# Start addresses of TensorE's operands in SBUF: streamed tiles at 0 and held tiles at 128 modulo 256 bytes, in place of 0 and 64 modulo 128

## The chip, the cores and the metric

The kernel runs on one core of a Trainium2 chip. The metric is the device time of one execution in microseconds (us), and the time of a kernel is the median of several executions. TensorE (PE in the profile) multiplies, with its weight loads shown apart as PEld. VectorE (DVE), ScalarE (ACT) and GpSimd (POOL) do the elementwise work, and SyncE (SP) issues most of the DMAs.

## The reference

A gated linear attention over 4 batches, 8 heads, 768 steps and head size 48, followed by a two-layer feed-forward block with an exact GELU (3072 tokens, 384 wide, 2048 hidden). All arrays are float32.

```
state = 0                                   # [B, H, 48, 48]
for t in range(768):
    state = alpha[t, :, None] * state + outer(k[t], v[t])
    y[t] = q[t] @ state
x = y as [3072, 384]
h = x @ w_in                                # [3072, 2048]
g = 0.5 * h * (1 + erf(h / sqrt(2)))
out = g @ w_out                             # [3072, 384]
```

## The kernel before, in words

**Attention.** The 768 steps are cut into blocks of 256 tokens, 12 blocks in all, each with two units of four heads (24 units). In a unit VectorE makes running products of alpha by scans (L339, L352) and scales queries and keys with them. TensorE then makes scores (L379), the products inside a chunk of 64 steps (L469), the sums of keys and values (L488) and what the carried state adds (L546). These are float32 matmuls on 64 by 64 or 48 by 48 corners of the array. Their operands are the tiles `qd`, `kd`, `vn`, `ss`, `kn` and `states`.

**Feed-forward.** A float32 matrix is split into a high and a low part in the format float32r, and a product is made of three matmuls: high by high, low by high, high by low. The weights are `wih`, `wil` (w_in, high and low) and `woh`, `wol` (w_out). The attention's output, split, is the tile `x` (in the program's names `x0`, `x3`, `x4`, `x6`, `x10`, or `two_x`). Every matmul loads 128 columns of the one operand as weights and streams the other.

- Narrow blocks, 0 to 3, have 256 tokens. The first product (L665) holds `wih`/`wil` and streams 256 columns of `x`. Blocks 0 and 3 read `x0` and `x3`, blocks 1 and 2 `two_x`. The second product (L886) holds the GELU's output, `ghi` or `glo`, and streams 384 columns of `woh` or `wol`.
- Wide blocks, four of them, have 512 tokens. The first product (L681) holds `wih`/`wil` and streams 512 columns of `x` (blocks 4, 6 and 10) or `two_x` (block 8). The second product holds `woh`/`wol` and streams 512 columns of `ghi`/`glo` (L696).
- From the second wide block on most of the second product is made by a scheme with fewer multiplications (L790). It streams `ghi`/`glo` or a difference of them, which lies in the places of `qd0` and `ad1`. As weights it holds `woh`/`wol` or sums of those, which lie in room that other tiles left (`sums_x`, `sums_kn`, `sums_ss`, `sums_z`, `sums_pp`, `sums_rp`, and the tiles `x0`, `qd1`, `kd1`).

In the program these are 576 matmuls of L665 (256 columns), 384 of L886 (384 columns), 432 of L681 on `x4`, `x6` and `x10` and 144 on `two_x`, 180 of L696 (512 columns each), and 132 of 512 and 462 of 256 columns of L790: 2,310 in all. Each is issued right behind the last one. The weights of the next one are loaded while this one streams.

**Order.** A planner in the kernel places every step by a table of costs (`COST`) and due times and writes out the order of all engines by hand. Addresses don't enter it. Tiles lie in SBUF pools in the order in which they are asked for, and `gap` asks for an unused tile where an address is to be moved on.

**Addresses.** A tile begins at the same byte in every one of the 128 partitions. `gap(pool, name, size)` takes `size % LINE` bytes. Before, `LINE` is 128 and the offsets are these:

```
STREAM, HELD, X_AT = 0, 64, 0
LINE = 128
```

Of the kernel before, what the change touches and what calls it, by code (L numbers as in the profile page):

```python
# [8 lines left out]
F32 = mybir.dt.float32  # L9
F32R = mybir.dt.float32r  # L10
# [33 lines left out]
    hi=0.82, lo=0.89, gemm1=2.12, gelu=0.51, low=0.62, most=1.4, last=0.69, part=1.0,  # L44
    wide1=2.1, wide2=2.07, wpart=1.1, quick1=2.45, quick2=1.42, comb1=0.36, comb3=1.08, chi=0.98, clo=1.2, wsum=0.72, wcomb=0.52, whi=0.52, wlo=0.65, gather=1.7, keep=0.95, evac=1.45, wend0=1.38, wend1=2.76, fsum=0.4, fall=0.2, fout=0.2,
)
STREAM, HELD, X_AT = 0, 64, 0
LINE = 128
ORDER = "0 1 a b c 2 d 3 e f 4 g h i j k 5 l m n o p"


# [1 line left out]
def gla_then_gelu_ffn(ctx: ExitStack, tc: tile.TileContext, q, k, v, alpha, qg, kg, ag, vg, w_in, w_out, out):  # L53
    nc = tc.nc
    B, H, D, S = q.shape
    NF, P, NK, _ = w_in.shape
    DM, DFF = NK * P, NF * P
    NT = B * S
    C = 128
    G = 2 * C  # L60
# [13 lines left out]
    A_MAX = 1.04  # L74
    MID, BOTTOM = 2.0**53, 2.0**-80

    def gap(pool, name, size):

        if size % LINE:
            pool.tile([C, size % LINE // 4], F32, tag=f"gap_{name}", bufs=1, name=f"gap_{name}")  # L80

    const = ctx.enter_context(tc.tile_pool(name="const", bufs=1))
    work = ctx.enter_context(tc.tile_pool(name="work", bufs=3))
    ffn = ctx.enter_context(tc.tile_pool(name="ffn", bufs=2))
# [5 lines left out]
    first = first_cm.__enter__()  # L90
# [27 lines left out]
    W = 2 * G  # L118
# [43 lines left out]
    bottom = column("bottom", BOTTOM).to_broadcast([P, G])  # L162
    outside = const.tile([P, 3 * NG * NU], F32, name="outside")
    ends = const.tile([P, NG * NU, 2], F32, name="ends")
    gap(const, "data", STREAM - 64)

    NB = 2

    def data_tile(n, i, dtype=F32):
        return const.tile([P, NPAIR, G], dtype, tag=f"{n}d{i}", name=f"{n}d{i}")  # L170

    vbuf = []
    data = []
    for i in range(NB):
        vbuf.append(const.tile([P, NCH, HV * D + DR], F32, name=f"vn{i}"))
        data.append({"a": data_tile("a", i)})
        gap(const, f"k{i}", (HELD - STREAM) * i)
        data[i].update({n: data_tile(n, i) for n in "kq"})

    states = []  # L180
    for u in range(NU):
# [29 lines left out]
    parts_all = const.tile([P, NSB, 2, DM], F32, name="parts")  # L211
    parts = [parts_all[:, i] for i in range(NSB)]
    LONG = NK * 2 * G
    gap(const, "x0", X_AT - HELD)
    x0_room = const.tile([P, LONG + LINE // 4], F32R, name="x0")
    x0 = x0_room[:, :LONG].rearrange("p (n h t) -> p n h t", n=NK, h=2)
    gap(const, "minus", HELD - X_AT)

    edge = ctx.enter_context(tc.tile_pool(name="edge", bufs=1, side="right"))
    gap(edge, "edge", 96 - X_AT)  # L220
    stage_cm = tc.tile_pool(name="stage", bufs=STAGE, side="right")
    stage = stage_cm.__enter__()
    late = []
# [35 lines left out]
    minus = const.tile([P, P], F32R, name="minus")  # L259
# [303 lines left out]
    def block_of(g):  # L563
        return next((pair for pair in WIDE if g in pair), g)

    later = []

    def x_pool():
        if not later:
            early_cm.__exit__(None, None, None)  # L570
            later.append(ctx.enter_context(tc.tile_pool(name="later", bufs=1)))
            gap(later[0], "two_x", X_AT - STREAM)
        return later[0]

    def two_x():
        if len(later) < 2:
            later.append(x_pool().tile([P, NK * 2 * W], F32R, name="two_x"))
        return later[1]

    def x_tiles(g):  # L580
        pair = block_of(g)
        if pair == g:
            if g == NSB:
                x = late[0].tile([P, LONG + LINE // 4], F32R, tag="xn", bufs=1, name=f"x{g}")
                x = x[:, :LONG].rearrange("p (n h t) -> p n h t", n=NK, h=2)
            else:
                x = x0 if g in (0, "s") else two_x().rearrange("p (g n h t) -> p g n h t", g=2, n=NK, h=2)[:, g - 1]
            xt[g] = x[:, :, 0], x[:, :, 1]
            return x
        if pair not in xt:  # L590
            if pair == WIDE[2]:
                x = two_x().rearrange("p (n j h t) -> p n j h t", n=NK, j=2, h=2)
            else:
                x = late[0].tile([P, NK, 2, 2, G], F32R, tag="xl", name=f"x{g}")
            xt[pair] = x
        h = pair.index(g)
        return xt[pair][:, :, h]
# [19 lines left out]
    def x_tile(g):  # L617
        if (g, "x") not in cur:
            cur[g, "x"] = x_tiles(g)
            if g:  # L620
                cur[g, "z"] = ffn.tile([P, 2, G], F32R, tag="z", bufs=1, name=f"z{g}")
            else:
                cur[g, "z"] = ffn.tile([P, 2, G], F32, tag="z", bufs=1, name="z0")[:, 0]
# [90 lines left out]
    rooms = []  # L714

    def room_of():

        if not rooms:
            x3 = late[0].tile([P, LONG + LINE // 4], F32R, tag="xn", bufs=1, name="sums_x")
            first = (HELD - X_AT) % LINE // 4  # L720
            rooms.extend(x[:, first + i * 2 * G : first + (i + 1) * 2 * G] for x in (x0_room, x3) for i in range(NK))
        elif len(rooms) == 2 * NK:
            for n, i in (("q", 1), ("k", 1)):
                x = taken(n, i).rearrange("p n t -> p (n t)")
                rooms.extend((x[:, : 2 * G], x[:, 2 * G :]))
            for pool, tag, bufs in ((work, "kn", 2), (work, "kn", 2), (work, "ss", 1), (ffn, "z", 1), (work, "pp", 1), (work, "rp", 1)):
                rooms.append(pool.tile([P, 2 * G], F32R, tag=tag, bufs=bufs, name=f"sums_{tag}"))
        return rooms[2 * len(sums) : 2 * len(sums) + 2]
# [6 lines left out]
    def taken(n, i):  # L735
        quick.setdefault("taken", []).append((n, i))
        return data_tile(n, i, F32R)

    def w_sums(f2):
        places = room_of()  # L740
        sums[f2] = [x.rearrange("p (n e) -> p n e", n=4) for x in places]
        nc.vector.tensor_tensor(
            out=plain[:, :4].rearrange("p (f e) c -> p f (e c)", f=2),
            in0=wo_hi[f2][:, :, : 2 * P].bitcast(F32),
            in1=wo_lo[f2][:, :, : 2 * P].bitcast(F32),
            op=ALU.add,
        )
# [162 lines left out]
    def general_path():  # L910
# [77 lines left out]
        def narrow_block(n0):  # L988
            x = x_tiles("s")
            for c in range(2):  # L990
                x_again(x, n0, c, slice(c * C, (c + 1) * C))
            acc = [ps_o().tile([P, DM], F32, tag=f"acc{t}", name=f"acc{t}_s") for t in range(2)]
            for f in range(NF2):
                hp = gemm1("s", f)
                gh = gelus("s", f, hp)
                gl = gelu_low("s", f, hp, gh)
                evacuate = gemm2("s", f, gh, gl, acc, f == 0, f == NF2 - 1, f == NF2 - 1, n0)
            evacuate()
# [207 lines left out]

    total = const.tile([P, 1], F32, name="total")
    flag = const.tile([1, 1], I32, name="flag")
    gap(const, "work", HELD)
    gap(ffn, "ffn", STREAM - HELD)  # L1210

    def flag_sum():
        nc.vector.tensor_scalar(
# [353 lines left out]
    t = 0.0  # L1567
    idle = 0
    while True:
# [17 lines left out]
        t = min(later_on)  # L1587
# [92 lines left out]
```

## Time and profile before

| | |
|---|---|
| median of 3 executions | 482.35 us (482.22 to 483.43) |
| the profiled execution | 482.24 us |
| its span, first to last instruction | 480.7 us |
| TensorE busy | 470.0 us, 98% of the span |
| TensorE's weight loads busy | 412.3 us |
| VectorE busy | 340.6 us, 71% |
| ScalarE busy | 228.2 us, 47% |
| share of TensorE in the chain that ended last | 93% |

The chain that ended last is followed back from the last instruction of the program. Each of its pieces names the engine, the tile written, the line and the number of instructions. Where matmuls stand back to back in it, the length of a piece divided by its count is the time from the start of one matmul to the start of the next. I call that the spacing. The time that the profile gives for one matmul alone is longer than the spacing, since matmuls are pipelined.

### The profile page before, as it was taken

What the parts mean: (1) busy time and instruction counts of PE and PEld (TensorE: products, weight loads), DVE (VectorE), ACT (ScalarE), POOL (GpSimd) and SP (SyncE); (2) the same over time, 40 slices, a digit from 0 to 9 for tenths busy, and PEclk for the clock granted to TensorE, in tenths of its full rate; (3) what the DMA queues carried; (4) which work ended last, traced back from release to release, by engine and by line L of the source; (5) the groups of instructions that cost most, each with busy time, mean ns of one, the idle gap of its engine ahead of it and who ended that gap; (6) DMA issues with size and microseconds to landing.
All of it is one profiled execution on the core that took longest, in us unless ns stands there. A gap on an engine that the chain in (4) does not pass through costs nothing.

```text
span 480.7 us, 12552 instructions
## 1 busy us (share of the span) xinstructions
PE 470.0 (98%) x5328; PEld 412.3 (86%) x5328; DVE 340.6 (71%) x666; ACT 228.2 (47%) x429; POOL 7.4 (2%) x21
## 2 busy tenths in 40 slices
PE   7999999999999999999999999999999999999994
PEld 5688999999999999887778878888888888888883
DVE  6899899987977978788882354797474545654542
ACT  5898676353544344535343244454443343523341
POOL 2000000000000000000000000000000000000000
PEclk9999999999999999999999999999999999999998
DMA  7997654557656554646340040000010000010002
GB/s 298 400 388 244 220 180 167 166 174 188 219 169 192 175 171 148 195 148 214 96 148 10 22 138 31 1 0 1 1 65 2 1 0 1 0 67 0 2 1 73
DMA packets 33921, 56.68 MB, mean 118 GB/s; under 512 B 3744, under 2 KB 13280, under 8 KB 33856
## 3 DMA queue, kind: packets, MB, share of 16 engines
q1 hardware_dynamic: 32400, 50.94, 32.3%
q0 software_dynamic: 880, 3.93, 2.1%
q8 instruction: 44, 0.72, 0.6%
q10 hardware_dynamic: 576, 0.92, 0.5%
q14 instruction: 21, 0.17, 0.1%
HBM read 43.45 MB, written 12.32 MB: 116 GB/s over the span
## 4 chain that ended last, share of the span: by engine, by line
PE 93%; DVE 3%; DMA 1%; issue 1%; ACT 0%; SPq 0%; DVEq 0%
PE hw L681 28%; PE acc L886 14%; PE hp L665 13%; PE accw L790 11%; PE accw L696 9%; PE sbank L790 6%; PE sbank L469 2%; PE sbank L546 2%; PE sbank L488 2%; DMA two_x<-zd 1%; PE sh L379 1%; DVE pp L339 1%; PE ybank L546 1%; DVE rp L352 1%; PE sbank L379 1%
## 5 line engine op out<-in xcount | busy, mean ns | idle before, releaser
L681 PE MATMUL hw<-x,wih 128*128 128x512 f32 x288 | 89.8, 393 | 0.0
L861 ACT ACTIVATE ghi<-hw 128x512 fp32r<-128x512 f32 x64 | 38.2, 597 | 91.0 <-PE hw L681 88.8
L876 DVE TENSOR_TENSOR glo<-h,ghi 128x512 fp32r<-128x512 f32 x44 | 30.1, 688 | 52.9 <-ACT h L866 52.9
L681 PEld LDWEIGHTS hw<-x,wih 128*128 128x128 f32 x288 | 52.0, 188 | 9.9
L681 PE MATMUL hw<-x,wil 128*128 128x512 f32 x144 | 56.6, 393 | 0.0
L783 ACT CAST qd<-ad 128x1024 fp32r<-128x1024 f32 x22 | 23.1, 1052 | 45.6 <-DVE ad L780 45.6
L886 PE MATMUL acc<-woh,ghi 128*128 128x384 f32 x128 | 44.1, 344 | 0.0
L886 PE MATMUL acc<-wol,ghi 128*128 128x384 f32 x128 | 43.0, 336 | 0.0
L786 DVE TENSOR_TENSOR ad<-ad,qd 128x1024 fp32r<-128x1024 f32 x22 | 26.9, 1224 | 18.7 <-ACT qd L783 18.7
L861 ACT ACTIVATE ghi<-hp 128x512 fp32r<-128x512 f32 x32 | 19.1, 596 | 42.5 <-PE hp L665 42.3
L665 PE MATMUL hp<-x,wih 128*128 128x256 f32 x192 | 35.0, 282 | 0.0
L665 PE MATMUL hp<-two_x,wih 128*128 128x256 f32 x192 | 34.4, 281 | 0.4 <-DMA two_x<-zd 0.4
L352 DVE TENSOR_TENSOR_SCAN rp<-ad,rp,bottom 128x255 f32<-128x255 f32 x48 | 34.1, 739 | 0.9
L339 DVE TENSOR_TENSOR_SCAN pp<-ad,bottom 128x256 f32<-128x256 f32 x48 | 30.7, 666 | 3.7 <-DMA ad<-in_ag_dram 3.7
L681 PEld LDWEIGHTS hw<-x,wil 128*128 128x128 f32 x144 | 27.0, 188 | 6.1
L665 PEld LDWEIGHTS hp<-two_x,wih 128*128 128x128 f32 x192 | 29.8, 188 | 0.6 <-PE hp L665 0.6
L681 PE MATMUL hw<-two_x,wih 128*128 128x512 f32 x96 | 30.1, 395 | 0.0
L665 PEld LDWEIGHTS hp<-x,wih 128*128 128x128 f32 x192 | 29.7, 188 | 0.2
L876 DVE TENSOR_TENSOR glo<-hw,ghi 128x512 fp32r<-128x512 f32 x20 | 13.8, 688 | 21.4 <-ACT hw L866 21.2
L886 PE MATMUL acc<-woh,glo 128*128 128x384 f32 x128 | 28.4, 344 | 0.0
L665 PE MATMUL hp<-two_x,wil 128*128 128x256 f32 x96 | 26.9, 280 | 0.0
L665 PE MATMUL hp<-x,wil 128*128 128x256 f32 x96 | 26.7, 280 | 0.0
(268 smaller groups left out, 1105.6 us busy)
## 6 DMA issues: line engine op xcount, KB each, us to landing
st<-in_moe_w_in_dram SPq DMA_DIRECT2D x8, 768.0 KB, 7.5
st<-in_moe_w_out_dram SPq DMA_DIRECT2D x8, 768.0 KB, 6.5
qd<-in_qg_dram SPq DMA_DIRECT2D x23, 256.0 KB, 3.5
ad<-in_ag_dram SPq DMA_DIRECT2D x23, 256.0 KB, 3.6
kd<-in_kg_dram SPq DMA_DIRECT2D x23, 256.0 KB, 4.5
vn<-in_vg_dram SPq DMA_DIRECT2D x12, 416.0 KB, 6.3
fd<-fl SPq DMA_DIRECT2D x18, 256.0 KB, 2.1
kx<-fd SPq DMA_DIRECT2D x72, 64.0 KB, 3.2
```

The lines of the kernel that those rows point to most:

```text
L339: nc.vector.tensor_tensor_scan(pp[:, i], at[:, i], bottom, MID, ALU.mult, ALU.max)
L352: nc.vector.tensor_tensor_scan(rp[:, i, G - 2 :: -1], at[:, i, G - 1 : 0 : -1], bottom[:, 1:], rp[:, i, G - 1 :], ALU.mult, ALU.max)
L546: ins = nc.tensor.matmul(ybank[o, i, t], lhsT=states[u][r, j, i], rhs=d["qt"][r, i, t], start=False, stop=True, skip_group_check=True,)
L665: nc.tensor.matmul(hp[:, j, :], lhsT=a[:, j, i * P : (i + 1) * P], rhs=x[:, i, :], start=(start and m == 0), stop=(stop and (j, i, n) in t ...
L681: nc.tensor.matmul(hp, lhsT=a[:, j, i * P : (i + 1) * P], rhs=x[:, i, :, part], start=(i == 0 and n == 0), stop=(i == NK - 1 and n == 2),)
L696: nc.tensor.matmul(acc[i], lhsT=w[:, j, e], rhs=a, start=(f == 0 and k == 0 and w is wo_hi[f2]), skip_group_check=mixed, stop=(f == NF - 1 ...
L783: nc.scalar.copy(quick["hi"], quick["t"])
L786: nc.vector.tensor_tensor(out=quick["lo"], in0=quick["t"], in1=quick["hi"].bitcast(F32), op=ALU.subtract)
L790: nc.tensor.matmul(to, lhsT=a[x], rhs=b[y], start=(start and n == 0), stop=True, skip_group_check=True)
L861: nc.scalar.activation(ghi, hp, AF.Gelu)
L876: nc.vector.tensor_tensor(out=glo, in0=hp, in1=ghi.bitcast(F32), op=ALU.subtract)
L886: nc.tensor.matmul(acc[t], lhsT=a[:, j, t * C : (t + 1) * C], rhs=w[:, j, :], start=(first and j == 0 and k == 0 and w is wo_hi[f]), stop= ...
```

## The change

It renames and refines the offsets, makes them count modulo 256 bytes, and puts gaps where they are needed for it. The core of the diff:

```diff
-STREAM, HELD, X_AT = 0, 64, 0
-LINE = 128
+LINE = 256
+GELU_AT, HELD_AT, COMB_AT, WIDE_AT, NARROW_AT = 0, 128, 0, 0, 0
...
-    gap(const, "data", STREAM - 64)
+    gap(const, HELD_AT - 192)
...
-        data.append({"a": data_tile("a", i)})
-        gap(const, f"k{i}", (HELD - STREAM) * i)
-        data[i].update({n: data_tile(n, i) for n in "kq"})
+        data.append({})
+        for n in "akq":
+            if (n, i) in (("q", 0), ("a", 1)):
+                gap(const, (COMB_AT - HELD_AT) * (i == 0))
+            data[i][n] = data_tile(n, i)
+            if (n, i) == ("a", 1):
+                gap(const, HELD_AT - COMB_AT)
...
-    gap(const, "x0", X_AT - HELD)
-    x0_room = const.tile([P, LONG + LINE // 4], F32R, name="x0")
-    x0 = x0_room[:, :LONG].rearrange("p (n h t) -> p n h t", n=NK, h=2)
-    gap(const, "minus", HELD - X_AT)
+    def long_tile(pool, name, **kw):
+        return pool.tile([P, LONG + LINE // 4], F32R, name=name, **kw)
+
+    def narrow_x(t):
+        at = (NARROW_AT - HELD_AT) % LINE // 4
+        return t[:, at : at + LONG].rearrange("p (n h t) -> p n h t", n=NK, h=2)
+
+    x0_room = long_tile(const, "x0")
+    x0 = narrow_x(x0_room)
...
-    gap(edge, "edge", 96 - X_AT)
+    gap(edge, 224 - WIDE_AT)
...
-            gap(later[0], "two_x", X_AT - STREAM)
+            gap(later[0], WIDE_AT - GELU_AT)
...
-            later.append(x_pool().tile([P, NK * 2 * W], F32R, name="two_x"))
+            later.append(x_pool().tile([P, 2 * LONG + LINE // 4], F32R, name="two_x"))
...
-            first = (HELD - X_AT) % LINE // 4
-            rooms.extend(x[:, first + i * 2 * G : first + (i + 1) * 2 * G] for x in (x0_room, x3) for i in range(NK))
+            rooms.extend(x[:, i * 2 * G : (i + 1) * 2 * G] for x in (x0_room, x3) for i in range(NK))
...
-    gap(const, "work", HELD)
-    gap(ffn, "ffn", STREAM - HELD)
+    gap(const, -64)
+    gap(ffn, GELU_AT - HELD_AT)
```

The order of instructions stays as it is: on each of the five engines the two programs agree row by row. Only addresses move. This is where tiles begin modulo 256 bytes, from the two built programs (slices that matmuls take of a float32r tile are whole multiples of 512 bytes apart, so that they keep its residue):

| tile | used as | before | after |
|---|---|---|---|
| `wih`, `wil`, `woh`, `wol` | weights (L665, L681, L696, L790), streamed in L886 | 64 | 128 |
| `ghi`, `glo` | streamed (L696, L790), weights in L886 | 0 | 0 |
| `x4`, `x6`, `x10` | streamed (L681) | 128 | 0 |
| `two_x` | streamed (L665, L681) | 0 | 0 |
| `x0` as streamed | L665, block 0 | 128 | 0 |
| `x3` as streamed | L665, block 3 | 0 | 0 |
| `qd0`, `ad1` | streamed differences (L790) | 0 | 0 |
| sums in `x0`, `sums_kn`, `sums_ss`, `sums_pp`, `sums_rp` | weights (L790) | 192 | 128 |
| sums in `sums_x`, `qd1`, `kd1` | weights (L790) | 64 | 128 |
| `sums_z` | weights (L790, 8 matmuls) | 0 | 0 |
| `kd0`; `states0`; `states1` | weights of small float32 matmuls | 0; 64; 192 | 128; 128; 0 |

The distance that the text below speaks of is the start of the weights that are being loaded less the start of what streams meanwhile, modulo 256. Over the pairs of float32r matmuls that follow each other in the order, it is before 64 in 1,194 of them, 192 in 1,039, 0 in 40 and 128 in 3. After the change it is 128 in 2,233 and 0 in 43.

## Rows read from the trace of the kernel before

**Rows 1.** The page: busy us and share of each engine; TensorE in 40 slices.

```profile
PE 470.0 (98%) x5328; PEld 412.3 (86%) x5328; DVE 340.6 (71%) x666; ACT 228.2 (47%) x429; POOL 7.4 (2%) x21
PE   7999999999999999999999999999999999999994
```

**Rows 2.** TensorE's waits: for whom, us in total, times, longest.

```profile
PE sfirst L150 <- POOL ident masks.py:199: 1.7, 1, 1.7
PE spare L379 <- DVE kd L358: 0.8, 1, 0.8
PE sbank L488 <- issue: 0.7, 1, 0.7
PE ybank L469 <- ACT kn L440: 0.4, 1, 0.4
PE hp L665 <- DMA two_x<-zd: 0.4, 1, 0.4
```

**Rows 3.** Windows, all engines: stretch, us, PE, PEld, DVE, ACT, POOL, clock, DMA.

```profile
12.00:60.00 48.00, 46.28 (x721) 40.90 (x719) 44.26 (x73) 38.70 (x70) 0.00 (x0) 1.00 0.87 313
120.00:180.00 60.00, 60.00 (x1025) 57.50 (x1018) 49.73 (x105) 27.83 (x60) 1.46 (x2) 1.00 0.59 185
360.00:420.00 60.00, 60.00 (x336) 51.96 (x335) 31.37 (x58) 24.34 (x41) 0.00 (x0) 1.00 0.00 1
```

**Rows 4.** The chain that ended last: start us, us, what; 512 columns streamed.

```profile
208.34 4.12 PE hw L681 x18
255.59 4.19 PE accw L696 x18
350.18 4.19 PE hw L681 x18
354.37 0.70 PE accw L790 x3
424.28 0.69 PE accw L790 x3
```

**Rows 5.** The same chain, 384 and 256 columns streamed, before 150 us.

```profile
90.34 4.16 PE acc L886 x24
132.55 4.24 PE hp L665 x36
```

**Rows 6.** The same chain, the new scheme's 256-column matmuls.

```profile
348.77 1.06 PE sbank L790 x9
356.80 1.02 PE sbank L790 x9
420.81 1.06 PE sbank L790 x9
428.79 1.02 PE sbank L790 x9
```

**Rows 7.** Instructions by tile: count, duration in ns (least/median/most), first and last start.

```profile
L681 PE MATMUL hw<-two_x,wih x96: 388/393/398, 342.0 to 404.2; 128*128 128x512 f32 x96
L886 PE MATMUL acc<-wol,ghi x128: 332/336/341, 26.6 to 195.4; 128*128 128x384 f32 x128
L665 PE MATMUL hp<-x,wil x96: 276/280/286, 21.4 to 190.7; 128*128 128x256 f32 x96
L790 PE MATMUL sbank<-qd,sums_z x6: 277/281/285, 348.7 to 413.5; 128*128 128x256 f32 x6
L790 PE MATMUL sbank<-qd,sums_pp x6: 276/278/280, 356.6 to 421.4; 128*128 128x256 f32 x6
```

**Rows 8.** The chain: small float32 matmuls against the states.

```profile
138.19 0.59 PE ybank L546 x32
148.83 0.60 PE sbank L546 x32
```

More of the change, by code (lines that the diff above doesn't have):

```diff
@@ L75, in gla_then_gelu_ffn, with gap @@
     MID, BOTTOM = 2.0**53, 2.0**-80
-    def gap(pool, name, size):
+    gaps = []
+    def gap(pool, size):
         if size % LINE:
-            pool.tile([C, size % LINE // 4], F32, tag=f"gap_{name}", bufs=1, name=f"gap_{name}")
+            n = f"gap{len(gaps)}"
+            gaps.append(pool.tile([C, size % LINE // 4], F32, tag=n, bufs=1, name=n))
     const = ctx.enter_context(tc.tile_pool(name="const", bufs=1))
@@ L576, in two_x, with both_x @@
         if len(later) < 2:
-            later.append(x_pool().tile([P, NK * 2 * W], F32R, name="two_x"))
+            later.append(x_pool().tile([P, 2 * LONG + LINE // 4], F32R, name="two_x"))
         return later[1]
+    def both_x(at):
+        at = (at - WIDE_AT) % LINE // 4
+        return two_x()[:, at : at + 2 * LONG]
     def x_tiles(g):
@@ L583, in x_tiles @@
             if g == NSB:
-                x = late[0].tile([P, LONG + LINE // 4], F32R, tag="xn", bufs=1, name=f"x{g}")
-                x = x[:, :LONG].rearrange("p (n h t) -> p n h t", n=NK, h=2)
+                x = narrow_x(long_tile(late[0], f"x{g}", tag="xn", bufs=1))
+                gap(late[0], WIDE_AT - HELD_AT)
             else:
-                x = x0 if g in (0, "s") else two_x().rearrange("p (g n h t) -> p g n h t", g=2, n=NK, h=2)[:, g - 1]
+                x = x0 if g in (0, "s") else both_x(NARROW_AT).rearrange("p (g n h t) -> p g n h t", g=2, n=NK, h=2)[:, g - 1]
             xt[g] = x[:, :, 0], x[:, :, 1]
@@ L591, in x_tiles @@
             if pair == WIDE[2]:
-                x = two_x().rearrange("p (n j h t) -> p n j h t", n=NK, j=2, h=2)
+                x = both_x(WIDE_AT).rearrange("p (n j h t) -> p n j h t", n=NK, j=2, h=2)
             else:
@@ L718, in room_of @@
         if not rooms:
-            x3 = late[0].tile([P, LONG + LINE // 4], F32R, tag="xn", bufs=1, name="sums_x")
-            first = (HELD - X_AT) % LINE // 4
-            rooms.extend(x[:, first + i * 2 * G : first + (i + 1) * 2 * G] for x in (x0_room, x3) for i in range(NK))
+            x3 = long_tile(late[0], "sums_x", tag="xn", bufs=1)
+            rooms.extend(x[:, i * 2 * G : (i + 1) * 2 * G] for x in (x0_room, x3) for i in range(NK))
         elif len(rooms) == 2 * NK:
```

## The prediction

> **What bounds the kernel now.** I read the page first. TensorE is busy 470.0 us of the span, and only the first and the last of the 40 slices lie below nine tenths [rows 1]. Its waits come next: the five longest sum to 4.0 us of the span [rows 2]. The windows say where another engine could bind. From 12 to 60 us VectorE is busy 44.26 of 48 us. Later TensorE fills its windows and VectorE has 10 to 29 us to spare in each 60 [rows 3]. The granted clock there is 1.00, so these matmuls run at the upper level, 2.4 GHz. So from about 60 us on, the time is the sum of the spacings of matmuls, and the question is how long one spacing is.
>
> The chain answers it. Eighteen matmuls of L681 on `x` take 4.12 us, 228.9 ns each. Eighteen on `two_x` take 4.19 us, 232.8 ns each, and so do eighteen of L696 [rows 4]. All stream 512 columns and load 128 by 128 weights. They differ in where operands begin: with `x` the distance from data to weights is 192 (data at 128, weights at 64), with `two_x` and `ghi` it is 64. For 256 columns there are two spacings: nine matmuls take 1.02 us (113.3 ns each) or 1.06 us (117.8 ns), and L665 takes 4.24 us for 36 (117.8 ns) [rows 5, 6]. For 384 columns it is 4.16/24 = 173.3 ns [rows 5].
>
> **A floor.** The shortest stretch is 1.02 us for nine times 256 columns. By columns, this makes 170.0 ns for 384 and 226.7 ns for 512. The least durations support the scaling: 276, 332 and 388 ns, 56 ns for each 128 columns more [rows 7]. Every matmul loads the same 128 columns of weights, so a time that grows with the streamed columns alone isn't the loading. What lies above the floor can be, and that is all that I let the change touch:
>
> - L681 on `x`: 432 times 2.2 ns, 0.95 us
> - L681 on `two_x`: 144 times 6.1, 0.88 us
> - L696: 180 times 6.1, 1.10 us
> - L790, 512 columns: three take 0.70 or 0.69 us [rows 4], about 231.7 ns; 132 times 5.0, 0.66 us
> - L886: 384 times 3.3, 1.27 us
> - L665: 576 times 4.5, 2.59 us
> - L790, 256 columns: both spacings occur; taken half and half, 462 times 2.25, 1.04 us
>
> Together 8.5 us. It is the most that another placement of the operands can give here.
>
> **The change part by part.** No instruction is added, removed or moved, and no wait. It changes addresses, and 2,233 of 2,276 neighbouring pairs get distance 128. The trace of before has three such pairs among 2,276, so no row prices it, and I bound it from both sides.
>
> *From above (gain).* All of it goes to the floor: 8.5 us.
>
> *From below (loss).* Distance 0 is the nearest row on the bad side. Matmuls with `sums_z` (weights at 0 under data at 0) have a median of 281 ns, the same matmuls with `sums_pp` (at 192) 278 ns [rows 7]. If 128 were as bad as 0, the loss would be about 3 ns on each of 2,310 matmuls, 6.9 us.
>
> *What I take.* At 512 columns the distance plainly counts: 64 costs 6.1 ns, 192 costs 2.2 ns, and 0 is the worst by the row above. If the pattern repeats every 256 bytes, 128 is the place farthest from 0. I take for it the middle between the floor and the better row: 1.1 ns over the floor at 512 columns, half of today's 3.3 at 384. At 256 columns the distance isn't all. The same weights `sums_pp` and `sums_rp`, at 192, run at 113.3 ns from 356.80 us and at 117.8 ns from 420.81 us [rows 6], so a train of matmuls seems to keep the rhythm with which it was entered. There I take half of L665 for the short spacing, as L790 shows it today, and leave L790 as it is. The gain is then 432 x 1.1 + 144 x 5.0 + 180 x 5.0 + 132 x 3.9 + 384 x 1.65 + 576 x 2.25 ns = 0.48 + 0.72 + 0.90 + 0.51 + 0.63 + 1.30 = 4.5 us.
>
> *What of it is kept.* Before 60 us VectorE sets the pace [rows 3], and about a tenth of the gain (the first blocks' L665 and L886) goes into waits: 0.4 us. Later nothing else is late today, but a faster TensorE will meet some results of ScalarE and VectorE that now come just in time. I take 15% off for that, 0.6 us. This leaves 3.5 us.
>
> *The rest.* The small float32 matmuls move too, and I cost them at nothing: 32 matmuls of L546 take 0.59 us where `states0` and the data begin at the same residue (unit 10) and 0.60 us where `states1` lies 128 further (unit 11) [rows 8]. VectorE's, ScalarE's and the DMAs' tiles move by multiples of 32 bytes. If that cost 1% of VectorE's 44.26 us before 60 us, 0.4 us would show, and nothing afterwards, where it has time to spare. I take 0.
>
> **Sum.** 482.24 us of the profiled execution (span 480.7 and 1.5 around it) less 3.5 gives 478.7 us. The median of before, 482.35, is 0.1 above that execution, which I neglect.
>
> **A rule weighed against rows.** The same instruction with the same shapes has 228.9 or 232.8 ns by where its operand begins [rows 4]. The Trainium skill (TensorE: Matmul & The Clock Gate, Part 2, "Step-by-step: what each phase is for") says that TensorE has two independent SBUF read ports, one for the streamed operand and one for the weights, and that loading the next weights takes no read bandwidth from the running matmul. By that rule an address changes nothing, and the time stays at 482.24 us. The rows at 512 columns speak against it, since they differ by 3.9 ns for equal work. But they are rows of different blocks, so what differs could be the rhythm in which each was entered. I keep this as the first rival.
>
> **The rivals.**
>
> 1. *Addresses don't decide it; 128 is worth the mean of 64 and 192.* The spacing comes from the rhythm of a train. For it: 113.3 and 117.8 ns with the same weights [rows 6], and 512-column rows that come from different blocks. Against it: the two rows of L681 [rows 4]. Time: 482.24 us, within 1.4 us either way. Chance 0.27.
> 2. *The pattern repeats every 128 bytes, and distance 128 is the same as 0.* It is slower then. Every pair of before has 64 on a ring of 128 bytes, the best place, and would go to the worst. Price: up to 6.9 us (482.24 + 6.9 = 489.1), or half of it, 485.7 us, if only the part of the load that meets the stream's start suffers. It decides from 0.6 ns per matmul on (1.4 us over 2,310). For it: the row of `sums_z`. Against it: on such a ring 64 and 192 are one place, and they differ by 3.9 ns at 512 columns. Chance 0.19.
> 3. *All goes to the floor.* 482.24 - 8.5 = 473.7 us. It takes a distance at which the load never meets the stream. For it: no row at 128 speaks against it. Against it: a load of 512 bytes that runs beside a stream of 1,024 to 2,048 bytes passes every residue, whatever the start. Chance 0.09, a part of "faster".
>
> My forecast, a gain between 1.5 and 7 us, has 0.45.
>
> **Range and chances.** About 0.3% (1.45 us) is what a measurement of this kernel can tell from no change. Faster by more: 0.45 + 0.09 = 0.54. Within: 0.27. Slower: 0.19. The range goes from 474.5, which leaves out the best part of rival 3, to 485.5, which leaves out the worse half of rival 2. The likeliest case alone spans 475.2 to 480.8.
>
> **What would show it.** Right: the chain's pieces of L681, L696 and L665 shrink, eighteen of L681 to some 4.10 us on `x` and on `two_x` alike, 36 of L665 towards 4.16 us, with the busy time of VectorE and ScalarE unchanged. Rival 1: pieces of 4.12 and 4.19 us stay, only in other blocks. Rival 2: L665 above 4.3 us for 36, and 512 columns at 236 ns or more. I am wrong on what is kept if the pieces shrink and new waits of TensorE for ScalarE or VectorE take it back.

## The result: slower, 486.91 us, and the profile after

The changed kernel takes 486.91 us (median of 5, 485.26 to 487.0) against 482.65 us for the kernel before in the same comparison. The ratio is 1.008, with a 95% interval of 1.0062 to 1.0098. I had forecast 478.7 us and faster. The time lies outside my range, on the other side of no change.

The page of the changed kernel, with busy time and share of each engine:

```profile
span 485.3 us, 12552 instructions
PE 475.1 (98%) x5328; PEld 416.0 (86%) x5328; DVE 341.3 (70%) x666; ACT 228.1 (47%) x429; POOL 7.4 (2%) x21
PE   8999999999999999999999999999999999999994
```

Against [rows 1] TensorE is 5.1 us longer busy and no other engine moved by more than 0.7 us. The span grew by 4.6 us. So the time went into TensorE itself. Its five longest waits sum to 3.8 us, against 4.0 in [rows 2], though the one for `two_x` grew from 0.4 to 1.0. The three longest (for whom, us in total, times, longest):

```profile
PE sfirst L153 <- POOL ident masks.py:199: 1.7, 1, 1.7
PE hp L682 <- DMA two_x<-zd: 1.0, 1, 1.0
PE sbank L501 <- issue: 0.5, 1, 0.5
```

The chain of the changed kernel (start, us, what; line numbers have moved: L665 is now L682, L681 L698, L696 L713, L790 L806, L886 L902) answers to [rows 4 to 6]:

```profile
80.78 4.27 PE hp L682 x36
91.53 4.22 PE acc L902 x24
210.58 4.20 PE hw L698 x18
258.15 4.17 PE accw L713 x18
344.13 1.06 PE sbank L806 x9
352.21 1.06 PE sbank L806 x9
353.64 4.17 PE hw L698 x18
360.28 1.07 PE sbank L806 x9
```

The pieces of 4.12 us are gone: eighteen of the wide first product now take 4.17 to 4.20 us on every x tile. The nine at 1.02 us are gone too, and those of 384 columns went from 4.16 to 4.22 us. The short spacings have vanished and the long ones have become the rule.

This table gives the mean time over the floor (113.3, 170.0 and 226.7 ns), in ns per matmul. I worked it out from the starts of all float32r matmuls in each trace, leaving out those behind which TensorE waited (spacings over 1.15 floors and 3 ns). The last row multiplies each mean by the number of matmuls that went into it and adds up. The other columns belong to experiments below; "chosen" is the placement chosen from the map.

| group (columns) | before | after | held at 0 | held at 64 | held at 192 | chosen |
|---|---|---|---|---|---|---|
| L665 on `two_x` (256) | 3.7 | 5.6 | 6.3 | 3.9 | 4.4 | 0.3 |
| L665 on `x0`, `x3` (256) | 4.2 | 5.4 | 6.3 | 3.3 | 3.9 | 0.4 |
| L886 (384) | 3.7 | 5.9 | 4.0 | 3.9 | 5.3 | 3.9 |
| L681 on `x` (512) | 3.1 | 5.8 | 2.0 | 6.3 | 2.6 | 1.2 |
| L681 on `two_x` (512) | 6.0 | 5.8 | 2.9 | 6.2 | 2.3 | 1.4 |
| L696 (512) | 6.0 | 5.7 | 2.1 | 6.6 | 2.9 | 1.9 |
| L790 (512) | 4.5 | 6.9 | 2.9 | 5.5 | 2.8 | 3.0 |
| L790 (256) | 2.7 | 5.4 | 5.5 | 3.6 | 4.5 | 4.4 |
| sum, us | 8.5 | 12.8 | 9.4 | 10.3 | 8.5 | 5.0 |

The sum rises by 4.3 us from before to after, nearly the 4.6 us of the span. After the change each group has 5.4 to 6.9 ns over its floor, whatever its number of columns.

### The profile page after: what moved, and what is told of

Its sections match the earlier page's. It is cut to its first block, busy times and chain, and to the rows that moved or that the text cites. A ratio compares the mean times of both kernels' runs of the same rounds, so it can differ in the third digit from the quotient of the medians.

```text
span 485.3 us, 12552 instructions
## 1 busy us (share of the span) xinstructions
PE 475.1 (98%) x5328; PEld 416.0 (86%) x5328; DVE 341.3 (70%) x666; ACT 228.1 (47%) x429; POOL 7.4 (2%) x21
## 4 chain that ended last, share of the span: by engine, by line
PE 94%; DMA 4%; DVE 1%; ACT 1%; issue 0%; SPq 0%; ACTq 0%
PE hw L698 28%; PE acc L902 14%; PE hp L682 14%; PE accw L806 11%; PE accw L713 9%; PE sbank L806 6%; PE sbank L482 2%; DMA st<-in_moe_w_out_dram 2%; PE sbank L559 2%; PE sbank L501 2%; DMA two_x<-zd 1%; PE sh L392 1%; PE ybank L559 1%; PE sbank L392 1%; DMA ad<-in_ag_dram 0%; PE ybank L392 0%
## 5 line engine op out<-in xcount | busy, mean ns | idle before, releaser
L698 PE MATMUL hw<-x,wih 128*128 128x512 f32 x288 | 90.6, 396 | 0.0
L698 PEld LDWEIGHTS hw<-x,wih 128*128 128x128 f32 x288 | 52.2, 188 | 10.3
L698 PE MATMUL hw<-x,wil 128*128 128x512 f32 x144 | 56.9, 395 | 0.0
L902 PE MATMUL acc<-woh,ghi 128*128 128x384 f32 x128 | 44.1, 345 | 0.0
L902 PE MATMUL acc<-wol,ghi 128*128 128x384 f32 x128 | 43.2, 338 | 0.0
L682 PE MATMUL hp<-two_x,wih 128*128 128x256 f32 x192 | 34.9, 283 | 1.0 <-DMA two_x<-zd 1.0
L682 PE MATMUL hp<-x,wih 128*128 128x256 f32 x192 | 35.3, 284 | 0.0
L698 PEld LDWEIGHTS hw<-x,wil 128*128 128x128 f32 x144 | 27.1, 188 | 6.3
L682 PEld LDWEIGHTS hp<-two_x,wih 128*128 128x128 f32 x192 | 30.0, 188 | 1.1 <-PE hp L682 1.1
L698 PE MATMUL hw<-two_x,wih 128*128 128x512 f32 x96 | 30.1, 395 | 0.0
L682 PEld LDWEIGHTS hp<-x,wih 128*128 128x128 f32 x192 | 29.9, 188 | 0.2
L902 PE MATMUL acc<-woh,glo 128*128 128x384 f32 x128 | 28.5, 344 | 0.0
L682 PE MATMUL hp<-two_x,wil 128*128 128x256 f32 x96 | 27.0, 282 | 0.0
L682 PE MATMUL hp<-x,wil 128*128 128x256 f32 x96 | 26.8, 282 | 0.0
```

Of the source, the lines that this page charges most:

```text
L682: nc.tensor.matmul(hp[:, j, :], lhsT=a[:, j, i * P : (i + 1) * P], rhs=x[:, i, :], start=(start and m == 0), stop=(stop and (j, i, n) in t ...
L698: nc.tensor.matmul(hp, lhsT=a[:, j, i * P : (i + 1) * P], rhs=x[:, i, :, part], start=(i == 0 and n == 0), stop=(i == NK - 1 and n == 2),)
L902: nc.tensor.matmul(acc[t], lhsT=a[:, j, t * C : (t + 1) * C], rhs=w[:, j, :], start=(first and j == 0 and k == 0 and w is wo_hi[f]), stop= ...
```

## The experiments

Three theories of why distance 128 is slow. **A**, the second rival of the prediction: the pattern repeats every 128 bytes, so 128 is the same as 0. **B**: it repeats every 256 bytes, and 128 is a bad place of its own. **C**: not the distance but the places count, or other things that moved along.

### Held tiles at 64, 192 and 0

Each changes one number of the changed kernel. The streamed tiles stay at 0. In the three, `HELD_AT` is 64, 192 and 0:

```diff
-GELU_AT, HELD_AT, COMB_AT, WIDE_AT, NARROW_AT = 0, 128, 0, 0, 0
+GELU_AT, HELD_AT, COMB_AT, WIDE_AT, NARROW_AT = 0, 64, 0, 0, 0
```

> The changed kernel with the held tiles at 64 in place of 128 modulo 256, all streamed tiles at 0: the distance from data to weights is 64 in 1,883 pairs of matmuls, 192 in 350 (L886's counterpart) and 0 in 43. Theory A (the pattern repeats every 128 bytes, 64 is its best place): the time comes back to that of the kernel before, 482 to 483.5 us, with the matmuls on x near the two_x spacing of before (233 ns for 512 columns). Theory B (the pattern repeats every 256 bytes, 128 its worst place): also faster than 486.9, but 64 and 192 need not agree, and 192 was the better one, so 483 to 485. Theory C (what counts is that weights begin at 128, or another thing that the change moved, small matmuls or VectorE): the pieces of float32r matmuls would not move together, and some of the 4.3 us stays.

Measured: 484.6 us, ratio to the kernel before 1.0043 (1.0029 to 1.0056).

> The same with the held tiles at 192: the distance is 192 in 1,883 pairs, 64 in 350. Theory A: the same as held at 64 but for the rhythm, 481 to 483.5 us. Theory B by the rows of before, where 512 columns had 2.2 ns over the floor at 192 and 6.1 at 64: faster than held at 64 by some 456 times 3.9 ns, 1.8 us, so 480 to 481.5.

Measured: 482.74 us, ratio 1.001 (1.0001 to 1.002).

> The same with the held tiles at 0, so that all 2,276 pairs have distance 0. Theory A: 0 and 128 are one place, so the time is that of the changed kernel within 0.3%, 485.5 to 488.3 us, and every float32r matmul has about 5.7 ns over its floor of 113.3, 170.0 or 226.7 ns. Theory B: 0 is another place than 128; the time differs from 486.9 by more than 1.5 us, to either side.

Measured: 483.69 us, ratio 1.0034 (1.0021 to 1.0046).

Held at 0 is 3.2 us faster than held at 128 by the medians, and the intervals of the two ratios (1.0021 to 1.0046 and 1.0062 to 1.0098) don't meet. By theory A the two should have been alike. At 64 the time is inside what B gave, 483 to 485, and above the 482 to 483.5 that A gave. A falls, and with it the mechanism of my second rival, though not its sign. At 192 the time is that of the kernel before, above the 480 to 481.5 us that B gave. The table shows why nobody wins: at distance 0 the 512-column matmuls come down to 2 or 3 ns over the floor and the 256-column ones go up to 5.5 to 6.3. At 64 it is the other way round. Three pieces of the chain with all held at 0 (36 of 256 columns, 119.4 ns each, and two times 18 of 512, 226.7 ns each):

```profile
69.90 4.30 PE hp L682 x36
257.10 4.08 PE accw L713 x18
261.18 4.08 PE hw L698 x18
```

### A map of the spacing

The program is this loop on fixed tiles, and nothing else of the kernel. A train is a row of equal matmuls back to back. The letter of a weight tile says its distance: a is 0, b 16, up to p at 240 bytes (`STEP` is 16). The starts `m` and `w` count floats of 4 bytes:

```python
def train(n, x, at, count):
    """`count` matmuls that stream n columns; their weights begin `LETTERS.index(x) * STEP` bytes past the data, modulo 256."""
    d = LETTERS.index(x) * STEP
    m, w = at // 4, (at + d) % 256 // 4
    for i in range(count):
        rhs = mv[:, m + i % 2 * 512 : m + i % 2 * 512 + n]
        lhs = wt[x][:, w + i // 2 % 2 * 128 : w + i // 2 % 2 * 128 + 128]
        nc.tensor.matmul(banks[i % 2][:, :n], lhsT=lhs, rhs=rhs, start=True, stop=True, skip_group_check=True)
```

> Another program, which leaves out the whole computation: trains of 24 float32r matmuls of 512, 256, 384 and 128 columns on fixed tiles, each train with one distance from data to weights, in steps of 16 bytes from 0 to 240 (letters a to p in the tile names), then again with the data moved by 64 and by 128 bytes. Theory A: the spacing at a distance d equals that at d + 128, with 0 and 128 at some 5.7 ns over the floor for each number of columns and the least near 64 and 192. Theory B: 128 stands out against 0. Both: moving data and weights together changes nothing. Theory C (absolute places): the trains with the data moved by 64 differ from those without at the same distance.

Windows of its trace, each cut at the starts of two matmuls twenty apart inside one train (stretch, us, busy time of TensorE, clock, DMA). In order: 512 columns at distance 0, 64, 128, 192 and 240, then 384 columns at 0, 64, 128 and 192, then 256 columns at 0, 64, 128 and 192. The count in brackets takes in matmuls that reach over an edge, so the spacing is the stretch over 20:

```profile
23.90:28.43 4.53, 4.53 (x21) 1.00 0.00 0
45.99:50.66 4.67, 4.67 (x22) 1.00 0.00 0
68.36:73.03 4.67, 4.67 (x21) 1.00 0.00 0
90.66:95.24 4.58, 4.58 (x22) 1.00 0.00 0
107.37:111.90 4.53, 4.53 (x22) 1.00 0.00 0
158.03:161.50 3.47, 3.47 (x22) 1.00 0.00 0
174.70:178.17 3.47, 3.47 (x22) 1.00 0.00 0
191.42:194.94 3.52, 3.52 (x22) 1.00 0.00 0
208.29:211.76 3.47, 3.47 (x22) 1.00 0.02 5
112.48:114.88 2.40, 2.40 (x23) 1.00 0.00 0
123.85:126.11 2.26, 2.26 (x22) 1.00 0.00 0
135.14:137.54 2.40, 2.40 (x23) 1.00 0.00 0
146.56:148.91 2.35, 2.35 (x22) 1.00 0.02 7
```

For 512 columns this is 226.5 ns at distance 0, 233.5 at 64 and at 128, 229.0 at 192, 226.5 at 240. For 384 it is 173.5 and only at 128 176.0. For 256 it is 120 at 0 and at 128, 113 at 64, 117.5 at 192. From the starts of all trains, in ns over the floor of the first table:

| columns | at the floor | up to 3.5 ns over | the rest |
|---|---|---|---|
| 512 | 0, 16, 240 | 176, 192 | 32 to 160, 208, 224: 5.5 to 7.7 ns over |
| 384 | none | 0 to 64, 96, 112, 176, 192, 240 | 80, 128, 144, 160, 208, 224: 5.5 to 7.3 |
| 256 | 64 in one of two trains | 208, and 224 in one of two | 0 to 48, 80 to 192, 240: 4.0 to 7.2 |

So theory B holds, with the number of columns beside it: 128 lies in the worst group for each of the three, and there is no place that is good for all. For 384 columns the floor of 170.0 ns, which I had scaled from the other lengths, is reached at no distance; the least is 173.3. For 128 columns all eight distances have 111.5 to 111.7 ns. With the data moved by 64 bytes, or by 128, the 512-column trains at one distance agree within 0.5 ns, but for one of 1.1 ns (at 0, where the first matmuls of the train are longer), so the distance counts and not the place. These trains also bear out the 256 bytes: at distance 192 the weights start 192 bytes after the data's residue in the first trains and 64 bytes before it in the moved ones, and all have 229 ns. Trains of 256 columns at one distance agree less well: 113.4 and 117.8 ns at 64, 120.0 and 118.7 at 128, 116.9 and 117.8 at 224, and within 0.3 ns at the other five. In the map each distance has a weight tile of its own. That it isn't the tile is shown by the kernel, where the same weights were held at 0, 64, 128 and 192.

### Everything 64 bytes further

```diff
-GELU_AT, HELD_AT, COMB_AT, WIDE_AT, NARROW_AT = 0, 128, 0, 0, 0
+GELU_AT, HELD_AT, COMB_AT, WIDE_AT, NARROW_AT = 64, 192, 64, 64, 64
```

> The changed kernel with every offset 64 bytes further: streamed tiles at 64, held tiles at 192. The distance stays 128 in 2,233 pairs. If only the distance counts, it is the changed kernel's time within 0.3%, 485.5 to 488.3 us, with some 5.7 ns over the floor in every group. If the places themselves count (held tiles at 128, or the small matmuls', VectorE's and ScalarE's tiles that moved along), it differs.

Measured: 487.2 us, ratio 1.0108 (1.007 to 1.0147). In its trace the sum over the floor is 12.7 us, as in the changed kernel (12.8), and no group differs by more than 0.12 ns. Theory C falls: with the distance kept, every place can move by 64 bytes, and the loss stays.

### One part undone

The first starts the wide blocks' x at 128, so that L681's counterpart has distance 0. The second lets x in the narrow blocks and the differences of L790 start at 64:

```diff
-GELU_AT, HELD_AT, COMB_AT, WIDE_AT, NARROW_AT = 0, 128, 0, 0, 0
+GELU_AT, HELD_AT, COMB_AT, WIDE_AT, NARROW_AT = 0, 128, 0, 128, 0
```

```diff
-GELU_AT, HELD_AT, COMB_AT, WIDE_AT, NARROW_AT = 0, 128, 0, 0, 0
+GELU_AT, HELD_AT, COMB_AT, WIDE_AT, NARROW_AT = 0, 128, 64, 0, 64
```

> The changed kernel with one part undone: the wide blocks' x tiles start at 128, where the held weights start, so that the 576 matmuls of L681's counterpart have distance 0; everything else keeps 128. By the spacing map (512 columns: 226.7 ns at distance 0, 233.6 at 128) this gives back 576 times some 6 ns, 3.4 us: 483 to 484 us, eighteen of these matmuls in 4.08 us. If instead equal residues collide (the reading of the prediction, by which 0 is the worst place), it is no faster than the changed kernel, 486.9 us or more.

Measured: 485.33 us, ratio 1.0049 (1.0029 to 1.0068). It gives back 1.6 us of the 3.4 expected. In the profiled execution (484.14 us) L681's counterpart came down from 5.8 to 3.0 ns over the floor on `x` and 4.0 on `two_x`, not to 0. Two pieces of this kernel's chain, where 18 at distance 0 stand before 18 at 128:

```profile
252.21 4.13 PE hw L698 x18
256.34 4.19 PE accw L713 x18
```

The starts inside the trains show why it isn't 4.08 us. The train at 252.21 begins with spacings of 224 to 237 ns and comes to 227 ns after ten matmuls. Where L681's counterpart stands in trains of nine between those of the scheme, they begin at 232 to 236 ns and come to 227 after six, or not at all, and a whole train has a mean of 230.3 or 231.6 ns.

> The changed kernel with the other part undone: x in the narrow blocks and the differences of L790 start at 64, so that 840 of the 256-column matmuls have distance 64, and 512 and 384 columns keep 128. By the map 256 columns take 117.8 or 113.3 ns at 64 and 118.7 at 128, by the rhythm in which a train is entered: L665 gains 0.9 to 3.0 us, the differences 0.2 to 1.4: 482.5 to 485.8 us. L681's counterpart stays at 233 ns.

Measured: 484.47 us, ratio 1.0046 (1.002 to 1.0072), inside what was expected. L665's counterpart has 1.9 to 2.9 ns over the floor, and L681's counterpart 6.4 to 6.9, so it stays at 233 ns.

### A placement chosen from the map

Distance 0 where 512 or 384 columns stream, 64 where 256 columns of `x` or of the differences do; 198 matmuls that stream 256 columns of `ghi` or `glo` have 0. The second has 192 in place of 64, the third moves `ghi` and `glo` 64 bytes further:

```diff
-GELU_AT, HELD_AT, COMB_AT, WIDE_AT, NARROW_AT = 0, 128, 0, 0, 0
+GELU_AT, HELD_AT, COMB_AT, WIDE_AT, NARROW_AT = 128, 128, 64, 128, 64
```

```diff
-GELU_AT, HELD_AT, COMB_AT, WIDE_AT, NARROW_AT = 0, 128, 0, 0, 0
+GELU_AT, HELD_AT, COMB_AT, WIDE_AT, NARROW_AT = 128, 128, 192, 128, 192
```

```diff
-GELU_AT, HELD_AT, COMB_AT, WIDE_AT, NARROW_AT = 0, 128, 0, 0, 0
+GELU_AT, HELD_AT, COMB_AT, WIDE_AT, NARROW_AT = 192, 128, 64, 128, 64
```

> A placement chosen for each number of columns from the spacing map: distance 0 where 512 columns stream (L681, L696 and part of L790) and in L886, 64 where 256 columns stream from x or from the differences (L665, part of L790); the 198 matmuls of L790 that stream 256 columns of ghi or glo get 0 with them. Against the changed kernel: L681 -3.3 us, L696 -1.0, L790 with 512 columns -0.9, L886 -1.0, L665 -1.0, differences of L790 -0.7, ghi in L790 +0.3: 479.3 us, some 0.6% faster than the kernel before. If the map doesn't hold inside the kernel, where ScalarE, VectorE and DMAs use SBUF as well, or if TensorE then waits, it stays at 481 to 483.

Measured: 479.39 us, ratio 0.9929 (0.9907 to 0.9952). It beats the kernel before by 0.7%, and its median is 1.5% below that of the changed kernel. The chain of this kernel:

```profile
69.12 4.08 PE hp L682 x36
90.01 4.17 PE acc L902 x24
206.73 4.08 PE hw L698 x18
253.63 4.08 PE accw L713 x18
346.21 1.06 PE sbank L806 x9
347.62 4.08 PE hw L698 x18
354.14 1.04 PE sbank L806 x9
```

These pieces of eighteen 512-column matmuls are at 4.08 us, 226.7 ns each, and the narrow first product takes 4.08 us for 36, 113.3 ns, in all its trains but the first (117.9 ns). Not all 512-column trains are at the floor, and the table has means of 1.2 to 3.0 ns over it: of L681's counterpart, half of the trains of nine between those of the scheme take 229.7 ns per matmul. The nine matmuls of the scheme take 1.04 to 1.06 us: there a train at 64 stands between others at 0.

That the time comes out within 0.1 us of the 479.3 expected is partly luck. By the table, against the changed kernel, L665's counterpart gained 2.9 us in place of 1.0, and the 512-column groups 3.8 in place of 5.2. Against the kernel before, the sum over the floor fell by 3.5 us and the span by 2.5. Two waits of TensorE are longer than in [rows 2], by 0.5 and 0.7 us:

```profile
PE spare L392 <- DVE kd L371: 1.3, 1, 1.3
PE hp L682 <- DMA two_x<-zd: 1.1, 1, 1.1
```

> The same, but with distance 192 in place of 64 where 256 columns stream. The map gives 117.8 ns for 256 columns at 192, and 113.4 or 117.7 at 64 in two trains: by it 479.3 to 481 us, not faster than with 64.

Measured: 482.64 us, ratio 1.0002 (0.9984 to 1.002). That is 1.6 us above the upper end of what I gave, since L665's counterpart stays at 4.1 to 4.3 ns over the floor and the scheme's matmuls at 4.7.

> The placement chosen from the map, but with ghi and glo 64 bytes further, so that what streams them has distance 192 and not 0 (512 columns: 228.8 ns for 226.7; 256 columns: 117.8 or 113.3 for 120), and L886 has 64 (173.3 for 173.3). By the map 312 matmuls lose up to 2.1 ns, 0.7 us, and 198 gain 2.2 or 6.7 ns, 0.4 or 1.3 us: within 0.7 us of the placement with 0, 478.7 to 480.1 us, unless L665's trains fall into the long rhythm, which costs 576 times 4.4 ns, 2.5 us more.

Measured: 482.7 us, ratio 1.0006 (0.9992 to 1.002). The exception that I had named came true, though it is not all of the 3.3 us between the two kernels: by the starts, L665's counterpart makes 1.9 us, the 512-column groups 1.2 (those of L790 went from 3.0 to 6.8 ns over the floor, where the map had let me expect some 2). L665's counterpart runs at 4.24 us for 36 again, 117.8 ns, though its own distance is still 64, as the chain of this kernel shows:

```profile
69.32 4.24 PE hp L682 x36
```

What changed for it is the train before it, L886's counterpart, which now has distance 64 in place of 0. Behind that one all of its trains have 113.3 ns in the chosen kernel, and all but one have 117.8 here.

### The rhythm of a train

Two more programs of trains on fixed tiles, built like the map:

> Trains of 30 matmuls of 256 columns again, without the kernel's computation, at the distances 64, 192, 208, 224 and 128, each behind eight different short trains (512 columns at distance 0, 128 and 64, 384, 128 columns, 256 columns at distance 128 and 0). If a train keeps the rhythm in which it was entered, one distance shows two spacings (113.3 and 117.8 ns at 64 and at 192) by what ran before it. If the distance alone decides, all eight trains of one distance have one spacing.

At 64 four of the eight trains have 113.3 ns and four 117.8. At 192 two have 113.3 and six 117.8. At 208 all have 116.7, at 224 five have 116.7 and three 117.8, at 128 all some 118.7. Five windows, cut 26 matmuls apart (two trains at 64, two at 192, one at 128):

```profile
24.20:27.26 3.06, 3.06 (x28) 1.00 0.00 0
33.69:36.63 2.94, 2.94 (x28) 1.00 0.00 0
65.81:68.75 2.94, 2.94 (x28) 1.00 0.00 0
70.26:73.32 3.06, 3.06 (x28) 1.00 0.00 0
176.81:179.90 3.09, 3.09 (x29) 1.00 0.00 0
```

At 64 and at 192 a train settles within a few matmuls into one of two rhythms and keeps it to its end. What ran before it picks the rhythm: behind six 512-column matmuls at 64 a train at 64 has 113.3 ns, behind seven of them 117.8.

> Trains without the kernel's computation, to settle why L665 ran in the short rhythm (113.6 ns) with the chosen placement and in the long one when ghi and glo lay 64 bytes further: 30 matmuls of 256 columns at distance 64, each behind 4, 8 or 12 matmuls of 384 columns at distance 0, 64, 128 or 192 (those of L886's counterpart). If the distance of the train before sets the rhythm, the trains behind distance 0 have 113.3 ns, whatever their count, and those behind 64 have 117.8. If the count or chance sets it, the spacings don't sort by distance. And 30 matmuls of 512 columns at distance 0 behind 6 or 9 at 128, 64 and 192, as L681's counterpart stands behind L696's in the kernel with one part undone: if they reach 226.7 ns only after several matmuls at 229 to 236, this is why that kernel gave back less than 3.4 us.

Four windows of it, 26 spacings each, 256 columns at distance 64 behind 384 columns: behind 4 matmuls at distance 0, behind 8 at 0, behind 4 at 64, behind 4 at 128.

```profile
23.23:26.18 2.95, 2.95 (x29) 1.00 0.00 0
28.04:31.10 3.06, 3.06 (x28) 1.00 0.00 0
37.90:40.96 3.06, 3.06 (x28) 1.00 0.00 0
52.74:55.68 2.94, 2.94 (x28) 1.00 0.00 0
```

My expectation half fails. Behind 384 columns at 128 and at 192 all six trains fall into the short rhythm, and behind 64 all three into the long one, which fits the kernel with `ghi` further on. But behind distance 0 it is short after 4 and long after 8 and 12, so the count plays a part, or chance, as each train was run once. In the chosen kernel trains behind 8, 12 and 24 such matmuls at distance 0 are short. So these programs show that the order matters, but not why the chosen kernel got the short rhythm. The 512-column trains at distance 0 start at the floor behind 192, and reach it after 3 to 9 matmuls at 224 to 236 ns behind 64 and 128. The same is seen in the kernel with the wide part undone, and is why it gave back half: its trains of nine or eighteen stand between others at 128 and spend part of their length settling.

## Why the prediction was wrong

**The step that failed** is "What I take". I read the pattern as a ring of 256 bytes, put 128 as "the place farthest from 0", called 0 the worst by the row of `sums_z` [rows 7], and took the middle between the floor and the better row. The ring is right, and all else in that step is not. At 512 columns 0 is among the best places (226.7 ns), and 128 costs 6.9 ns over the floor. The row of `sums_z` is of 256 columns, where 0 is bad (120 ns), and I carried it over to matmuls of another length. With no row at 128 I let a smooth curve stand for a measurement. The sum left 1.1 ns over the floor at 512 columns, 1.65 at 384 and 2.25 at 256; the trace after the change shows 5.7 to 6.9, 5.9 and 5.4 to 5.6. By the map's values at 128 the sum of the prediction would have been a loss: 432 x (6.9 - 2.2) + 144 x 0.8 + 180 x 0.8 + 132 x 1.9 + 384 x (6.0 - 3.3) ns = 3.6 us from 512 and 384 columns, and with 1.0 ns on 576 and 3.2 on 462 matmuls of 256 columns (118.8 ns) 2.1 us more, 5.7 in all. The measured 4.3 us is less, mainly because most 512-column groups in the kernel have 5.7 to 5.8 and not 6.9 ns (0.8 us), and because L681 on `x` had 3.1 and not 2.2 before (0.4 us).

**The bounds.** The loss bound, 6.9 us, held, but by luck: its 3 ns came from distance 0 at 256 columns, which says nothing of 128 at other lengths. The 8.5 us held as the most to be gained: the chosen placement brings the sum to 5.0 us, and no train settled below the floor. But the 1.27 us of L886 in it stood on a floor for 384 columns that was scaled and that no train of the map reaches.

**256 columns.** That a train keeps a rhythm once it has settled was right for the distances 64 and 192, and was shown apart. But I used it only to take L665 half and half. At 128 neither rhythm of 64 and 192 was seen: all trains have about 118.7 ns in the second program of trains, and 120.0 in one train of the first.

**What is kept, and the rest.** That the time is the sum of spacings from 60 us on was right: no wait of TensorE in the two lists grew by more than 0.6 us. What I took off for waits (1.0 of 4.5 us) the changed kernel can't test, since nothing was gained. In the chosen kernel 2.5 of 3.5 us arrive in the span. The small float32 matmuls at nothing: right. From the first to the last start of a group of 32, L546 and its counterpart take 448 to 450 ns in every group, before and after.

**The rivals.** The first (addresses don't decide) is refuted by the trains of the map: equal work takes 226.7 or 233.5 ns by the distance alone. The Trainium skill says that loading the next weights takes no read bandwidth from the running matmul (TensorE: Matmul & The Clock Gate, Part 2, "Step-by-step: what each phase is for"). The trace doesn't agree with what I had drawn from that, that an address changes nothing; whether bandwidth is what is lost, no run here shows. The second rival had the right sign and about the right time (485.7 us at half its price). Its mechanism was wrong, so the nearness is luck, and the signs that I had given for it (over 4.3 us for 36, 236 ns) weren't met: 4.27 us and 232 to 234 ns. The third asked for a distance that brings all to the floor. At 512 columns there is one, 0, which I had called the worst.

**What stays open.** Why the distance acts as it does, and what a train hands to the next. Nor do the runs tell whether the weights of the next matmul count or the matmul's own, since within a train both start at the same residue. Executions of one kernel differ by unequal amounts: 482.69 to 487.18 us with the narrow part undone, 485.9 to 489.32 with everything 64 bytes further, 483.52 to 483.84 with all held at 0. Rhythms that fall differently from one execution to the next could be behind it. A lower granted clock could be too: the longest execution of the first two kernels has 0.991 and 0.993, their others have 0.992 to 0.999. With one trace of each kernel, neither is shown.

## What to carry to other kernels

Where TensorE fills the time and its spacing lies a few per cent over the shortest one seen, look at the start of the weights being loaded less the start of the streamed operand, modulo 256 bytes, for each number of columns apart. Measure the distances in a small program of trains before moving any tile: here float32r wants 0 for 512 columns and 64 for 256 (if its train falls into the short rhythm), and a curve through two or three rows of a kernel gave the wrong sign. Then look at the order too: what runs before a train decides how long it takes to settle and, at 64, whether it gets the short or the long rhythm. So measure the whole kernel afterwards.

## What the runs showed of the hardware

- The shortest spacing in which a train settled is 113.3 ns for 256 float32r columns, 173.3 ns for 384 and 226.7 ns for 512, with the granted clock at 1.00. At 2.4 GHz a column per clock would make 106.7, 160.0 and 213.3 ns. The ratio is 17 to 16 for 256 and 512 columns and 13 to 12 for 384.
- Weights and data that start at the same residue modulo 256 bytes are among the best cases at 512 columns (226.7 ns, as at 16 and 240) and among the worst at 256 (120 ns).
- Of equal trains of 30 matmuls of 256 columns at distance 64, some settle at 113.3 ns and some at 117.8, within six matmuls, and keep that to the end. Trains of 512 columns at distance 0 came to 226.7 ns behind every train tried, after ten matmuls at the most.
- At 128 columns the distance made no difference: 111.5 to 111.7 ns at eight distances.
